# One 64x128 weight load and matmul in place of two 64x64 side by side, in a relu-squared attention followed by a GeGLU feed-forward

## The chip, the core and the metric

The kernel runs on one core of a Trainium2 chip. The metric is the device time of one execution in microseconds (us). It takes 410.21 us, the median of 3 runs (409.67 to 410.41). Matrix products run on TensorE (PE in the profile, its weight loads PEld), elementwise work on VectorE (DVE) and ScalarE (ACT), and most DMAs are issued from GpSimd (POOL) and SyncE (SP).

## The reference

Inputs are float32; the kernel casts to bfloat16 on load and sums in float32.

```python
# q, k, v: (8, 12, 448, 64)   w_gate, w_val: (768, 1536)   w_out: (1536, 768)
scores = (q @ k.T) / sqrt(64)                  # per batch and head, 448 x 448
attn   = maximum(scores, 0)**2 / 448
x      = (attn @ v), heads side by side        # (8*448, 768)
g, val = x @ w_gate, x @ w_val                 # (3584, 1536) each
out    = (gelu(g) * val) @ w_out               # (3584, 768), float32
```

## The kernel before

**Four quarter arrays.** Nearly all products go through the helper `mm` (line 249), which issues one `nc.tensor.matmul` with `tile_position=(64*row, 64*col)`. Weights are 64 rows by 64 columns, so the 128x128 array is used as four independent 64x64 tiles. `row` says which half of the 128 contraction rows (SBUF partitions) an instruction reads, `col` which half of the output partitions it writes. The text calls the two values of `row` the lower and the upper row half. Each matmul comes with one weight load of the same 64x64.

**The products.** For each batch b:

- *scores* (`add_scores`): a unit holds 64 keys for two heads, one head in each row half. Moving data is 448 queries (or 2 x 224). The two columns of a row half have different weights. The result `sp` is squared after a relu by ACT and DVE into `attnT`.
- *values* (`add_values`): one unit for a pair of heads. The two columns of a row half hold different heads, so both weights and moving data differ. The lower half runs seven steps, of two matmuls each, and the upper half seven more, later, onto the same PSUM bank. DVE scales the result into `xT`.
- *gate and value* (`add_gate_value`): for each 128 columns `fc` of the 1,536 and for gate (g=0) and value (g=1), six steps `dc` in the lower row half and six in the upper. A step is two matmuls, j = 0 and 1, which have the same moving data `xT[b][HALF[r], dc, :]` (448 tokens) and the two 64-column halves of the weight.
- *output* (`add_product`): seven products ("1" to "7") for each group of four 64-token chunks instead of eight, with sums of `uT` and of `w_out` made by DVE. The stationary operand is `uT` or a sum of it, two 64-token chunks in the two columns, and the moving data is 384 columns of the weight, the same for j = 0 and 1. There are 7 chunks of 64 tokens in a batch, so that in 4 of the 28 pairs of chunks the two belong to different batches and lie in different `uT` tiles.

Besides, in the first 43 us, the queries and keys of batches 0 and 1 are transposed on the PE with 128-row, 64-column tiles (lines 477 and 514); line 1082 warms the PE up with tiles of that shape, and before 30 us idle time is filled with 128x128 matmuls on constants (`fill`, line 435). Batches 2 to 7 are transposed by DMA.

**The order of the PE's work.** A planner (`run_plan`) with a cost for each operation writes out one order for the PE. It has two streams: PE0 for the lower row half and PE1 for the upper. Gate, value, output and values units go in with `then`: the upper half's steps follow after the lower half's, while the lower half already runs another unit. Scores units go in with `both`: the two row halves run them together. So at most times the two row halves are in different units, and often in different kinds of product. `wait_lower` lets the first upper step of a unit wait for the last lower one, since both add into the same bank. The planner's costs for a step (0.189 us for 448 columns, 0.1625 us for 384) aren't changed by the diff, and neither is the order that it makes.

## Time and profile before

| | |
|---|---|
| median of 3 runs | 410.21 us (409.67 to 410.41) |
| the profiled execution: its time, and its span from first to last instruction | 410.71 us, 408.7 us |
| PE busy | 397.6 us (97%), 8,693 matmuls recorded |
| PEld busy | 357.4 us (87%), 8,696 weight loads |
| DVE, ACT, POOL busy | 250.4, 224.8, 74.3 us |
| matmuls of gate and value / output / scores / values | 4,608 / 2,352 / 768 / 768 |
| granted TensorE clock, mean | 0.998 |

The profiled execution took 2.0 us more than its span and 0.5 us more than the median. The four quarter tiles run side by side, so that the busy time of a group (its union over time) is far less than its count by its mean; and a matmul's recorded duration (349 ns for 448 columns) includes its way through the array. How much PE time a step costs is read from the distance between the starts of two successive matmuls of one tile, 0.19 us for 448 columns.

### The profile page before, as it was taken

The numbers are of one execution on the slowest core, as the hardware profiler recorded it, in microseconds if no ns is written. First come the engines' busy times: TensorE is split into PE (matmuls) and PEld (weight loads), VectorE is DVE, ScalarE is ACT, GpSimd is POOL, SyncE is SP. The second block draws the span as 40 slices with busy tenths as digits, with TensorE's granted clock in tenths as the row PEclk, the third lists the DMA queues.
The fourth block names the chain that finished last, engine by engine and source line by source line (L and its number), as shares of the span: only waits on it lengthen the run. The fifth ranks groups of instructions, "written<-read, shape, count | busy, mean of one in ns | idle before, by whom it ended". The sixth has DMA issues, their size and how long they took to land.

```text
span 408.7 us, 18873 instructions
## 1 busy us (share of the span) xinstructions
PE 397.6 (97%) x8693; PEld 357.4 (87%) x8696; DVE 250.4 (61%) x422; ACT 224.8 (55%) x323; POOL 74.3 (18%) x120
## 2 busy tenths in 40 slices
PE   7899999999999999999999999999999999999993
PEld 3466889988998999999999999999999999999993
DVE  3886678666775757756668563776577464524251
ACT  5858762366757647677266752766456762222220
POOL 8655410203122122001310113200310000000000
PEclk9999999999999999999999999999999999999999
DMA  7999997889769898473995549954993400050005
GB/s 102 189 199 199 198 209 129 117 126 129 108 81 182 148 139 111 58 189 49 116 126 83 143 56 130 113 103 82 107 135 89 116 2 3 3 152 9 3 3 156
DMA packets 75279, 44.87 MB, mean 110 GB/s; under 512 B 36160, under 2 KB 71744, under 8 KB 75200
## 3 DMA queue, kind: packets, MB, share of 16 engines
q0 software_dynamic: 37152, 24.39, 45.1%
q1 hardware_dynamic: 37888, 19.08, 23.7%
q8 instruction: 68, 1.11, 1.2%
q10 hardware_dynamic: 160, 0.20, 0.2%
q14 instruction: 11, 0.09, 0.1%
HBM read 48.76 MB, written 11.01 MB: 146 GB/s over the span
## 4 chain that ended last, share of the span: by engine, by line
PE 94%; DMA 3%; POOL 1%; issue 0%; DVE 0%; ACT 0%; DVEq 0%; POOLq 0%
PE ff L249 84%; PE sp L249 8%; DMA qk<-in_k_dram 2%; DMA v<-in_v_dram 2%; POOL qk L303 1%; PE sp L514 1%; PE ff L435 1%; PE ff L514 1%; DVE uT L721 0%; ACT osb L899 0%; POOL ident masks.py:199 0%; POOL ident masks.py:197 0%; DVEq L721 0%; POOLq L1118 0%
## 5 line engine op out<-in xcount | busy, mean ns | idle before, releaser
L249 PE MATMUL ff<-xT,wv 64*64 64x448 bf16 x2304 | 251.6, 349 | 0.0
L249 PE MATMUL ff<-xT,wg 64*64 64x448 bf16 x2304 | 246.5, 349 | 0.0
L581 ACT ACTIVATE rl<-sp 128x896 bf16<-128x896 f32 x168 | 151.8, 919 | 64.0 <-PE sp L249 62.1
L249 PEld LDWEIGHTS <-wv 64*64 64x64 bf16 x2304 | 147.9, 106 | 10.8
L249 PEld LDWEIGHTS <-wg 64*64 64x64 bf16 x2304 | 147.7, 106 | 9.6
L721 DVE TENSOR_TENSOR uT<-gel,ff 128x448 bf16<-128x448 bf16 x96 | 59.5, 620 | 77.7 <-PE ff L249 67.7
L592 DVE TENSOR_TENSOR attnT<-rl 128x1792 bf16<-128x1792 bf16 (+1 forms) x98 | 92.3, 954 | 24.1 <-ACT rl L581 23.5
L716 ACT ACTIVATE gel<-ff 128x448 bf16<-128x448 f32 x96 | 52.0, 542 | 74.5 <-PE ff L249 73.5
L249 PEld LDWEIGHTS <-s 64*64 64x64 bf16 x1344 | 85.0, 107 | 2.1
L249 PE MATMUL ff<-attnT,v 64*64 64x448 bf16 (+1 forms) x768 | 83.5, 326 | 0.5 <-DMA v<-in_v_dram 0.4
L249 PE MATMUL sp<-qkT 64*64 64x448 bf16 (+1 forms) x768 | 75.2, 328 | 0.8 <-ACT qkT L485 0.6
L249 PE MATMUL ff<-wt,s 64*64 64x384 bf16 x672 | 64.4, 323 | 0.0
L249 PEld LDWEIGHTS <-uT 64*64 64x64 bf16 x1008 | 63.5, 107 | 0.8
L249 PE MATMUL ff<-wo,uT 64*64 64x384 bf16 x672 | 60.9, 323 | 0.0
L249 PE MATMUL ff<-wo,s 64*64 64x384 bf16 x672 | 57.6, 323 | 0.0
L249 PEld LDWEIGHTS <-v 64*64 64x64 bf16 x768 | 46.2, 107 | 4.4 <-issue 0.9
L899 ACT COPY osb<-ff 128x384 f32<-128x384 f32 x56 | 26.6, 478 | 35.5 <-PE ff L249 35.4
L249 PEld LDWEIGHTS <-qkT 64*64 64x64 bf16 x768 | 36.7, 106 | 7.0 <-issue 3.4
L318 POOL DMA_DIRECT2D v<-in_v_dram x48 | 30.1, 634 | 62.0 <-DVE uT L721 38.1
L648 DVE TENSOR_SCALAR xT<-ff 128x448 bf16<-128x448 f32 x48 | 29.9, 623 | 16.0 <-PE ff L249 15.6
L249 PE MATMUL ff<-wt,uT 64*64 64x384 bf16 x336 | 35.3, 323 | 0.0
L897 DVE TENSOR_TENSOR osb<-ff,osb 128x384 f32<-128x384 f32 x42 | 23.3, 556 | 17.4 <-PE ff L249 17.0
(36 smaller groups left out, 126.5 us busy)
## 6 DMA issues: line engine op xcount, KB each, us to landing
out_dram<-osb SPq DMA_DIRECT2D x54, 192.0 KB, 4.1
v<-in_v_dram POOLq DMA_DIRECT2D x48, 128.0 KB, 4.7
qk<-in_q_dram POOLq DMA_DIRECT2D x23, 224.0 KB, 5.4
qk<-in_k_dram POOLq DMA_DIRECT2D x23, 224.0 KB, 5.0
wg<-in_moe_w_gate_dram POOLq DMA_DIRECT2D x6, 384.0 KB, 10.6
wv<-in_moe_w_val_dram POOLq DMA_DIRECT2D x6, 384.0 KB, 11.6
wo<-in_moe_w_out_dram POOLq DMA_DIRECT2D x4, 576.0 KB, 14.9
qkT<-qkr SPq DMA_TRANSPOSE x36, 4.9
```

Source lines behind the costliest of these rows:

```text
L249: return nc.tensor.matmul(o, lhsT, rhs, start=start, stop=stop, skip_group_check=onto, tile_position=(P * row, P * col))
L303: op = load(4 * (h1 - h0) * S * D, lambda: nc.gpsimd.dma_start(tile_of(), src[b, h0:h1].rearrange("h (p c) d -> p h (c d)", c=SC)), deps, ...
L318: return nc.gpsimd.dma_start(v16[b, m][HALF[i], :, :, :], v[b, h0:h1].rearrange("h (p c) d -> p h c d", c=SC)[:, :, c0:c0 + VC, :])
L435: nc.tensor.matmul(t[:, :], warm[:, 0:128], warm[:, :], start=True, stop=True)
L514: nc.tensor.transpose(t[HALF[j], c, :], src[:, 2 * r + j, c, :], ident[:, :], tile_position=(0, P * j))
L581: nc.scalar.activation(duo["rl"][:, u % 2, :, :], box[0][:, :, 0:S], AF.Relu)
L592: nc.vector.tensor_tensor(a[:, part], duo["rl"][:, part], duo["rl"][:, part], op=ALU.mult)
L648: nc.vector.tensor_scalar_mul(xT[b][:, pr, :], box[0][:, 0:S], scalar1=out_scale)
L716: nc.scalar.activation(gel[b, fc][:, :], box[0][:, 0:S], AF.Gelu)
L721: u_op[b, fc].ins = nc.vector.tensor_tensor(uT[b][:, fc, :], gel.pop((b, fc))[:, :], box[0][:, 0:S], op=ALU.mult).ins
L897: ins = nc.vector.tensor_tensor(o, box[0][:, 0:OGS], o, op=ALU.add)
L899: ins = nc.scalar.copy(o, box[0][:, 0:OGS])
```

## The change

The two matmuls j = 0 and 1 of a gate, value or output step become one with a weight of 64 rows by 128 columns at column 0, which writes all 128 output partitions. The moving data, the PSUM banks, the sums and the order stay as they are. Output steps whose two chunks belong to different batches stay two matmuls of 64x64, since their stationary operand isn't one slice. Scores and values stay as they are.

```diff
 # add_gate_value, emit(r, dc)
-            for j in range(2):
-                ins = mm(box[0][HALF[j], 0:S], w[HALF[r], dc, o + P * j:o + P * (j + 1)],
-                         xT[b][HALF[r], dc, :], r, j, r == 0 and dc == 0, r == 1 and dc == KC - 1)
-            box[1] = ins
+            box[1] = mm(box[0][:, 0:S], w[HALF[r], dc, o:o + 2 * P],
+                        xT[b][HALF[r], dc, :], r, 0, r == 0 and dc == 0, r == 1 and dc == KC - 1)
 # add_product, emit(r, fc)
-            for j in range(2):
-                if isinstance(source, str):
-                    a = st["tile"][source][HALF[r], fc, HALF[j]]
+            if isinstance(source, str):
+                parts = [(slice(0, 2 * P), st["tile"][source][HALF[r], fc, :])]
+            else:
+                t, half = source
+                (b, c), (b1, _) = chunks[t]
+                if b == b1:
+                    parts = [(slice(0, 2 * P), uT[b][HALF[r], half * KH + fc, c * P:(c + 2) * P])]
                 else:
-                    t, half = source
-                    b, c = chunks[t][j]
-                    a = uT[b][HALF[r], half * KH + fc, c * P:(c + 1) * P]
-                ins = mm(box[0][HALF[j], 0:OGS], a, weight_of(name, fc)[HALF[r], :], r, j,
+                    parts = [(HALF[j], uT[b][HALF[r], half * KH + fc, c * P:(c + 1) * P])
+                             for j, (b, c) in enumerate(chunks[t])]
+            for j, (to, a) in enumerate(parts):
+                ins = mm(box[0][to, 0:OGS], a, weight_of(name, fc)[HALF[r], :], r, j,
```

## The prediction

> **What bounds the kernel now.** I read the page's busy times and the chain first, then the stages.

> ```profile
> PE 397.6 (97%) x8693; PEld 357.4 (87%) x8696; DVE 250.4 (61%) x422; ACT 224.8 (55%) x323; POOL 74.3 (18%) x120
> PE   7899999999999999999999999999999999999993
> PEclk9999999999999999999999999999999999999999
> PE 94%; DMA 3%; POOL 1%; issue 0%; DVE 0%; ACT 0%; DVEq 0%; POOLq 0%
> 100.00:200.00 100.00, 99.99 (x2266) 93.54 (x2263) 67.72 (x110) 64.62 (x91) 18.02 (x30) 1.00 0.76 117
> 335.00:400.00 65.00, 65.00 (x1474) 61.24 (x1467) 29.02 (x61) 16.86 (x32) 0.00 (x0) 1.00 0.10 27
> ```

> The last two lines are stages: length, then PE, PEld, DVE, ACT, POOL, granted clock, DMA. The PE bounds everything but the first 30 us, at full clock; no other engine is above two thirds in a stage. But a busy PE may be only partly filled, so I asked what the four tiles do inside it. The timeline of the PE (start, length, what, count; neighbours of one kind merged):

> ```profile
> 60.89 0.35 PE L249 MATMUL ff<-xT,wg 64*64 64x448 bf16 x2
> 60.98 0.38 PE L249 MATMUL ff<-xT,wv 64*64 64x448 bf16 x2
> 61.08 0.35 PE L249 MATMUL ff<-attnT,v 64*64 64x448 bf16 x2
> 61.17 0.38 PE L249 MATMUL ff<-xT,wv 64*64 64x448 bf16 x2
> 61.27 0.35 PE L249 MATMUL ff<-attnT,v 64*64 64x448 bf16 x2
> ```

> One row half runs gate/value (60.98, 61.17), the other another unit (60.89, 61.08, 61.27), each 0.19 us a step, two matmuls per step. Successive starts of output steps are 0.162 us apart (108.46, 108.62, 108.78), those of transposes of 128 columns 0.055, so a column streams in some 0.42 ns and the constant per matmul is 2 to 3 ns. With that price all 8,696 matmuls, four side by side (two for 128x64, one for 128x128), fill 387 us of the 408.7. From 100 to 400 us the tiles are over 99% filled: there is no hole to close.

> **What the change removes.** Of 4,608 gate/value and 2,352 output matmuls all but 144 are paired: batches meet inside a pair of chunks in 4 of 28 pairs; two of these are the first pair of their group, in products 1 and 2, two the second, in product 4, so (2+2+1+1) products x 24 matmuls. That leaves 3,408 fewer matmuls and as many fewer loads (8,696 to 5,288). It takes nothing off the path: a 64x128 matmul streams the same 448 or 384 columns and holds both tiles of its row half for the same 0.189 or 0.162 us. Issue isn't the limit (where four are ready they start within 0.01 us, as at 42.54), and loads lie under the matmuls. The wider load is bounded by the transposes: two 64-column loads every 0.055 us, so 128 columns in at most that, under 0.162. Zero, as long as loads are issued ahead. Waits, DMAs, other engines and the order don't move.

> **What it adds.** Until now all PE work after 43 us had one shape. Afterwards scores, values and straddling output steps are 64x64 and the rest 64x128. What does a change of shape cost? This trace has such changes early on, between 64x64 and 128x64 or 128x128:

> ```profile
> 41.17 0.35 PE L249 MATMUL ff<-xT,wv 64*64 64x448 bf16 x2
> 41.17 0.35 PE L249 MATMUL ff<-attnT,v 64*64 64x448 bf16 x2
> 41.36 0.35 PE L249 MATMUL ff<-xT,wv 64*64 64x448 bf16 x2
> 41.64 0.97 PE L514 MATMUL sp<-ident,qk 128*64 128x128 bf16 x28
> 42.54 0.38 PE L249 MATMUL ff<-xT,wv 64*64 64x448 bf16 x2
> 42.55 0.38 PE L249 MATMUL ff<-attnT,v 64*64 64x448 bf16 x2
> 42.76 0.35 PE L249 MATMUL ff<-xT,wg 64*64 64x448 bf16 x2
> ```

> The last 64x64 pair (41.36) has streamed its columns by 41.55; the transposes begin at 41.64, 0.09 later. Their group ends at 42.61; the last of 0.22 began at 42.39 and streamed by 42.44; the next 64x64 begins at 42.54, 0.10 later. It isn't a late input: loads, which otherwise start as the matmul before them starts, also first start at 41.64 and 42.54. Behind four 128x128 fills (12.44 to 13.48, the last begun at 13.10 and streamed by 13.31) the next 64x64 begins at 13.41, again 0.10 later. After the change the first step is 0.214 long instead of 0.189 (42.54 to 42.76): 0.025 of weight load lies bare (0.011 for 128x128). So a change of shape costs 0.092 + 0.025 = 0.117 us, in which all four tiles stand still, and from one change to the next instructions of one shape alone run.

> The order in which the kernel issues its matmuls, which the change keeps, has 36 changes of shape now and 1,042 with the pairs joined. The 1,006 new ones: 285 of the narrow runs are a values step or two of one row half, between wide steps of the other; some 130 are scores. Two terms:

> - standstill: 1,006 x 0.117 = 117.7 us;
> - lost overlap: a values step in one row half ran beside a gate step in the other; now they take turns. Adding up, run by run of one shape, the fill of its busiest tile gives 389.4 us now and 457.2 with the pairs joined: 67.8 us. As a check, some 300 values steps of (6 x 0.189 + 2 x 0.095)/8 = 0.166 us each alone make 50 us, about 63 straddling output steps of 0.162 another 10, and ragged ends of wide runs the rest.

> Sum 185.5 us, nearly all before 335 us: 906 of the changes come before the last scores, 46 behind the last values. On the profiled execution's 410.7 it makes 596.2, on the median 595.7; I take 596. Nothing covers it: the PE sets the end, and others, 250 us busy at most, only wait longer.

> No row shows a change of columns alone at 64 rows, so the price has bounds: from below nothing (if this isn't such a change), from above the row just used, with a bare load between 0 and 0.1 us (a recorded 128-column load takes 0.097): 0 and +160 to +225. A gain is excluded, since no row shows a column in under 0.42 ns. I take the upper end: the rows nearest to it, the same instructions in the same queue, show a stop both on going narrower and on going wider.

> [...]

> **Rivals.**

> *The stop holds only the row half that changes.* The 128-row shapes use both halves, so the rows above can't exclude that a column change stops one alone. Followed half by half, the order has 705 more changes, each 0.117 us in one of two halves that otherwise run on: 705 x 0.117 / 2 = 41 us; a walk through the order, halves waiting for each other's place, gives 47, or 36 without bare loads. Time 447 to 458, taken 458. For it: the halves keep their own pace (0.162 beside 0.189).

> *No stop for columns (not slower).* Only a joining or splitting of the row halves would empty the array; 64x64 and 64x128 in one half would follow each other as now. Price: 0.117 becomes 0. Place: all 1,006 changes. It decides if a change costs under 0.8 us / 1,006 = 0.8 ns. Then 410.2; two tiles that drift 0.03 us apart (60.98 shows 0.38 for a pair) would move together, worth 0.03 us at a unit's end, at most 1 us in all. Against it: loads in these rows weren't even prefetched.

> *Wide loads bound the steps.* If the two row halves' 128-column loads went one after the other at the recorded 0.106, a pair of steps would need 0.213: 1,152 gate/value steps per half x 0.024 + 624 output steps x 0.051 = +59 us, 470. Against it: the transposes' 0.055 for 128 columns.

> **How the numbers follow.** Standstill of the whole array 0.66 (596, its own range 571 to 635); one row half 0.16 (458); no stop 0.14; loads 0.04 (470). About 0.2% is what a measurement of this kernel can tell from no change, 0.8 us: of the no-stop case 0.09 falls within, 0.03 faster, 0.02 slower. Faster 0.03, same 0.09, slower 0.88. Range 445 to 635: it takes in the row-half and load cases and leaves out the no-stop case (0.14) and some tail.

> **What would show it.** In the profile of the changed kernel: 5,288 loads; a mixed stretch where a wide step's start comes 0.09 after the columns before it have streamed, with its load starting no earlier; a values pair never within a wide matmul's stream; PEld idle rising; a granted clock still at 1; the last 46 us of wide work growing only some 10 us (46 changes) to 56. If in the timeline values and gate steps still alternate at 0.09 us as at 60.89 to 61.27, the prediction is wrong, and if they do so with pauses in one half only, the row-half rival is right.

## The result and the profile after

The changed kernel takes 606.4 us (median of 4 runs, 603.18 to 608.17) against 410.3 before: 1.477 times as long, 95% interval 1.470 to 1.485. The profiled execution took 608.17 us, with a span of 606.3. 596 was predicted. Two things were not as told: the array clock did not stay at 1 (0.962 in the mean of the profiled execution), and the standstills were a little cheaper than priced.

From the page of the changed kernel: busy times and counts, PE and granted clock in 40 slices, and two groups (busy, mean ns | idle before).

```profile
PE 596.6 (98%) x5285; PEld 260.5 (43%) x5288; DVE 253.4 (42%) x422; ACT 228.0 (38%) x323; POOL 73.8 (12%) x120
PE   7999999999999999999999999999999999999996
PEclk9979999999859999999999999999998799999999
L249 PE MATMUL ff<-xT,wv 64*128 64x448 bf16 x1152 | 265.9, 352 | 0.0
L249 PEld LDWEIGHTS <-wv 64*128 64x128 bf16 x1152 | 94.8, 94 | 62.3 <-issue 32.0
```

5,288 loads are left, as counted. The PE still reads 98% busy, and DVE and ACT run as many instructions as before; PE busy time grew by 199 us while its instructions fell by 39%. Busy time hides what happened; the timeline of the PE in a mixed stretch shows it (start, length, what, count):

```profile
262.90 0.38 PE L249 MATMUL ff<-attnT,v 64*64 64x448 bf16 x2
262.91 0.56 PE L249 MATMUL sp<-qkT 64*64 64x448 bf16 x4
263.40 0.36 PE L249 MATMUL ff<-xT,wg 64*128 64x448 bf16 x1
263.69 0.38 PE L249 MATMUL ff<-attnT,v 64*64 64x448 bf16 x2
264.00 0.36 PE L249 MATMUL ff<-xT,wg 64*128 64x448 bf16 x1
264.00 0.50 PE L249 MATMUL ff<-wo,s 64*128 64x384 bf16 x2
264.20 0.35 PE L249 MATMUL ff<-xT,wg 64*128 64x448 bf16 x1
```

Before, gate and values steps of the two row halves started 0.09 us apart and overlapped. Now the gate step at 263.40 runs alone, the values step at 263.69 alone, the gate step at 264.00 with an output step of the other half, because both are wide. From 263.40 a step streams until 263.59, and the next shape starts at 263.69, 0.10 later; likewise 263.69, 263.88 plus a bare load, 264.00. The weight loads of the same stretch:

```profile
263.40 0.09 PEld L249 LDWEIGHTS <-wg 64*128 64x128 bf16 x1 [0.36 <-issue]
263.69 0.11 PEld L249 LDWEIGHTS <-v 64*64 64x64 bf16 x2 [0.20 <-issue]
263.99 0.09 PEld L249 LDWEIGHTS <-wg 64*128 64x128 bf16 x1 [0.20 <-issue]
```

No load is issued ahead across a change of shape, here or at any other at full clock in this trace: the first load of the new shape starts no sooner than 0.09 us after the columns before it have streamed. Where nothing changes, wide steps keep their pace, both halves at once:

```profile
101.32 0.35 PE L249 MATMUL ff<-xT,wv 64*128 64x448 bf16 x1
101.32 0.35 PE L249 MATMUL ff<-xT,wg 64*128 64x448 bf16 x1
101.51 0.35 PE L249 MATMUL ff<-xT,wv 64*128 64x448 bf16 x1
101.51 0.35 PE L249 MATMUL ff<-xT,wg 64*128 64x448 bf16 x1
```

The new part is the clock. Two stages of 50 us each (length, PE, PEld, DVE, ACT, POOL, granted clock, DMA):

```profile
100.00:150.00 50.00, 50.00 (x449) 22.01 (x445) 22.07 (x35) 21.77 (x31) 6.73 (x11) 1.00 0.58 90
150.00:200.00 50.00, 50.00 (x373) 19.14 (x371) 18.99 (x32) 18.20 (x25) 5.56 (x10) 0.80 0.47 76
```

In the second the PE is as busy, at a mean clock of 0.80, and issues 76 matmuls fewer. The trace's clock record has three stretches at half clock before the end, 10.2, 20.5 and 13.7 us long, 44.4 us in all; before there was none while the PE worked. The four executions follow their clock: 608.2 and 608.1 us at 0.962 and 0.965, 604.8 at 0.968, 603.2 at 0.971.

### The profile page after: what moved, and what is told of

It is laid out like the page before. It is cut to its first block, busy times and chain, and to the rows that moved or that the text cites. A ratio compares the mean times of both kernels' runs of the same rounds, so it can differ in the third digit from the quotient of the medians.

```text
span 606.3 us, 12047 instructions
## 1 busy us (share of the span) xinstructions
PE 596.6 (98%) x5285; PEld 260.5 (43%) x5288; DVE 253.4 (42%) x422; ACT 228.0 (38%) x323; POOL 73.8 (12%) x120
## 4 chain that ended last, share of the span: by engine, by line
PE 97%; DMA 1%; POOL 1%; issue 0%; ACT 0%; POOLq 0%
PE ff L249 87%; PE sp L249 9%; DMA qk<-in_k_dram 1%; PE sp L514 1%; POOL qk L303 0%; PE ff L435 0%; PE ff L514 0%; ACT osb L901 0%; POOL ident masks.py:199 0%; POOL ident masks.py:197 0%; POOLq L1120 0%
## 5 line engine op out<-in xcount | busy, mean ns | idle before, releaser
L249 PE MATMUL ff<-xT,wv 64*128 64x448 bf16 x1152 | 265.9, 352 | 0.0
L249 PE MATMUL ff<-xT,wg 64*128 64x448 bf16 x1152 | 263.4, 355 | 0.0
L249 PE MATMUL ff<-attnT,v 64*64 64x448 bf16 (+1 forms) x768 | 127.2, 358 | 0.1
L249 PEld LDWEIGHTS <-wv 64*128 64x128 bf16 x1152 | 94.8, 94 | 62.3 <-issue 32.0
L249 PEld LDWEIGHTS <-wg 64*128 64x128 bf16 x1152 | 93.9, 94 | 61.2 <-issue 31.7
L249 PE MATMUL ff<-wt,s 64*128 64x384 bf16 x336 | 74.9, 339 | 0.0
L249 PEld LDWEIGHTS <-s 64*128 64x128 bf16 x672 | 55.9, 96 | 39.8 <-issue 25.3
L249 PEld LDWEIGHTS <-v 64*64 64x64 bf16 x768 | 39.3, 106 | 77.9 <-issue 76.8
L249 PE MATMUL sp<-qkT 64*64 64x448 bf16 (+1 forms) x768 | 70.5, 353 | 1.1 <-ACT qkT L485 0.6
L249 PE MATMUL ff<-wo,uT 64*128 64x384 bf16 (+1 forms) x384 | 69.9, 330 | 0.0
L249 PE MATMUL ff<-wo,s 64*128 64x384 bf16 x336 | 64.3, 336 | 0.0
L249 PEld LDWEIGHTS <-uT 64*128 64x128 bf16 (+1 forms) x576 | 42.1, 98 | 36.1 <-issue 26.4
L249 PE MATMUL ff<-wt,uT 64*128 64x384 bf16 (+1 forms) x192 | 46.1, 375 | 0.0
L249 PEld LDWEIGHTS <-qkT 64*64 64x64 bf16 x768 | 21.9, 104 | 52.9 <-issue 50.6
L318 POOL DMA_DIRECT2D v<-in_v_dram x48 | 29.6, 622 | 102.1 <-DVE uT L719 62.9
## 6 DMA issues: line engine op xcount, KB each, us to landing
wg<-in_moe_w_gate_dram POOLq DMA_DIRECT2D x6, 384.0 KB, 10.2
```

The lines of the kernel that those rows point to most:

```text
L249: return nc.tensor.matmul(o, lhsT, rhs, start=start, stop=stop, skip_group_check=onto, tile_position=(P * row, P * col))
L318: return nc.gpsimd.dma_start(v16[b, m][HALF[i], :, :, :], v[b, h0:h1].rearrange("h (p c) d -> p h c d", c=SC)[:, :, c0:c0 + VC, :])
```

## Experiments

Five readings were at stake: a change of shape stops the whole array (the forecast); it stops only the row half that changes; column changes stop nothing; wide weight loads bound the steps; or each wide instruction is slower in itself (196 us / 3,408 = 0.058 each). Full-clock figures in the expectations use the price measured in the changed kernel's trace, 0.111 us for a change.

**The shapes by themselves.** A kernel with only PE work, in stretches of one pattern each. `narrow(r)` is two 64x64 side by side in row half r (0 is the lower), `wide(r)` one 64x128:

```diff
+    for i in range(100):    # C; A has narrow(0), narrow(1) and B wide(0), wide(1)
+        narrow(0, i % 8)
+        wide(1, i % 8)
+    ...                     # D to H likewise
```

> PE work alone, nothing of the reference is computed (the output is zeros): eight stretches of steps of 448 columns, one after the other. Steps take 0.189 us. A: 64x64 pairs, lower and upper half, 100 times; B: 64x128, both halves, 100 times; C: 64x64 pair in the lower half, 64x128 in the upper, 100 times; D: 64x64 in both halves, then 64x128 in both, 100 times; E: 200 times 64x128 in the lower half alone; F: 64x128 in both halves, then 128x128, 60 times; G: 64x64 in both halves, then a pair of 128x64, 60 times; H: a pair of 128x64, then 128x128, 60 times. Theory (a change of shape stops the whole array, some 0.094 us plus a bare load of 0.011 to 0.025): A 18.9, B 18.9, C 200 x 0.300 = 60, D 200 x 0.300 = 60, E 37.8, F and H some 35, G 36.7. Rival (the stop holds only the row half that changes): C 18.9, since neither half changes, D 60. Rival (no stop when only columns change): C 18.9, D 37.8, F 35, G 36.7, H 22.7. Rival (wide loads bound the steps): B 21 or more.

Three parts of its PE timeline: C at full clock, C later, and D:

```profile
56.20 0.36 PE L48 MATMUL hi<-x,w 64*128 64x448 bf16 x1
56.49 0.38 PE L44 MATMUL lo<-x,w 64*64 64x448 bf16 x2
56.80 0.36 PE L48 MATMUL hi<-x,w 64*128 64x448 bf16 x1
57.09 0.38 PE L44 MATMUL lo<-x,w 64*64 64x448 bf16 x2
...
70.08 0.55 PE L48 MATMUL hi<-x,w 64*128 64x448 bf16 x1
70.56 0.58 PE L44 MATMUL lo<-x,w 64*64 64x448 bf16 x2
71.08 0.55 PE L48 MATMUL hi<-x,w 64*128 64x448 bf16 x1
...
161.68 0.36 PE L48 MATMUL lo<-x,w 64*128 64x448 bf16 x1
161.69 0.36 PE L48 MATMUL hi<-x,w 64*128 64x448 bf16 x1
161.98 0.38 PE L44 MATMUL lo<-x,w 64*64 64x448 bf16 x2
161.98 0.38 PE L44 MATMUL hi<-x,w 64*64 64x448 bf16 x2
```

In C neither row half ever changes its shape: the lower is always 64x64, the upper always 64x128. Yet they take turns: 0.60 us from one wide step to the next, so 0.300 for a step and a change, 0.111 more than a step. That excludes the row-half rival and the no-stop rival at once. D has the same 0.60 a round with both halves filled. The joining of columns at 128 rows (H) and that of rows with columns kept (F, G) took 0.30 to 0.31 too. A and B each took 19.0 us for their 100 rounds: wide steps are no slower, at 0.19 us in both halves, and the last two readings fall as well.

The stages A, B, C at half clock, D at full clock and E (wide steps in the lower half alone):

```profile
17.83:36.87 19.04, 19.04 (x401) 11.61 (x401) 0.00 (x0) 0.00 (x0) 1.00 0.85 335
36.87:55.89 19.02, 19.02 (x204) 9.65 (x200) 0.00 (x0) 0.00 (x0) 1.00 0.01 2
60.80:152.00 91.20, 91.20 (x276) 21.14 (x274) 0.00 (x0) 0.00 (x0) 0.50 0.00 0
160.00:215.00 55.00, 55.00 (x546) 18.84 (x544) 0.00 (x0) 0.00 (x0) 1.00 0.00 1
216.00:254.00 38.00, 38.00 (x204) 18.80 (x201) 0.00 (x0) 0.00 (x0) 1.00 0.00 0
```

(Length, PE, PEld, DVE, POOL, granted clock, DMA.) Five microseconds into C the clock halved and stayed there until 7 us into D: a round of C then took 1.00 us (70.08 to 71.08). E keeps half the array streaming all the time (0.5 of it), D, from 159.8 us on, the whole array 0.63 of the time; both ran at full clock. C streams half the array 0.63 of the time, 0.31. So what the clock follows isn't the busy PE, at 100% in all three.

**Everything wide.** Scores merged, and values, score tails and straddling output steps doubled, so that no narrow shape is left after the transposes (here the last are at 48 us):

```diff
 # add_values, on top of the change; scores and straddling steps likewise
-                o = box[0][HALF[j], 0:S]
+                o = box[0][:, 0:S]
...
-                    ins = mm(o, v16[b, pr // 2][HALF[i], 2 * (pr % 2) + j, w + i, :], a, i, j,
+                    ins = mm(o, two(w + i), a, i, 0,      # 128 columns
```

> The changed kernel with every other 64x64 step wide too: scores of 448 columns merged, and the steps whose two columns have different moving data (values, score tails, straddling output steps) as two 64x128 matmuls one after the other, so these stream twice as long. Some operands are then not the reference's (a score's second 64 keys, values' second head), so the output isn't either; sizes, order and everything outside the PE stay. After 43 us no change of shape is left. The tiles' fill grows from 387 to 429 us. Theory (each change of shape stops the whole array): the 1,006 stops and the lost overlap go, 410 + 43 = 453 us, at full clock. Rival (stop in one row half only): 453 as well. Rival (a wide step itself costs more, 196 us / 3,408 = 0.058 each): about 720. Rival (lower clock because of the shape): over 470.

458.44 us (4 runs, 458.24 to 459.24), 1.117 times before (1.112 to 1.121). The array streams 42 us more than in the changed kernel, and the time is 148 us shorter. The forecast's mechanism gives 453; some 5 us are left over. By the trace the time in which any tile streams grew by 49 us where the forecast has 43; why isn't known. The cost of the change thus lies in mixing, not in wide steps. From its page:

```profile
PE 447.6 (98%) x4997; PEld 306.9 (67%) x5000; DVE 252.4 (55%) x422; ACT 226.2 (50%) x323; POOL 73.7 (16%) x120
PEclk9999999999999999999999999999999999999998
```

**Stops without lost overlap.** Only scores wide, in the kernel before:

```diff
 # add_scores, emit(j, pr)
+            if not tail:
+                mm(sp[:, j, 0:S].rearrange("k (c p) -> k c p", c=SC),
+                   t[:, cl, :], t[:, :, HALF[0]], j, 0, True, True)
+                return
```

> The kernel before, with only the 576 score matmuls of 448 columns merged into 288 of 64x128 (the second 64 keys are other columns than the reference's, so the output isn't either). Scores units run in both row halves together, so hardly any overlap is lost: the order has 267 changes of shape more, and the fill of the busiest tile, run by run, grows only from 389.4 to 393.4 us. Theory (whole array): 267 x 0.111 = 29.6 plus 4.0, 444 us. Rival (row half only): 439. Rival (cost by wide instruction, 288 x 0.058): 427. Rival (no stop): 410.

446.19 us, 1.087 times before (1.082 to 1.092), at full clock throughout. Against the 410.97 of the same chip that is 35.2 us for 267 changes, 0.132 each all told, or 0.117 after the 4.0 us of overlap that were expected. Added up from the trace, the time in which any tile streams grew by 8 us, not 4, which leaves 0.10 for each. Either way the standstill is a cost of its own.

**Half of the change.** Gate and value wide, output narrow:

```diff
 # add_product: as before; add_gate_value: as after
```

> Only the gate and value half of the change; output steps stay pairs of 64x64. Fewer instructions are wide (2,304 of 3,408), but output steps now are one more kind that the wide steps alternate with: 1,377 new changes in place of 1,006, and the fill run by run is 497.7 us (457.2 with the whole change, 389.4 before). Theory (whole array): 410 + 153 + 108 = 671 us at full clock, up to 4% more if the clock falls as it did with the whole change: slower than the whole change by 65 to 90. Rival (row half only): 453. Rival (cost by wide instruction): 543, faster than the whole change.

Four executions took 766.1, 767.3, 785.4 and 801.8 us, at granted clocks of 0.853, 0.849, 0.826 and 0.804. The two with the higher clock make 1.867 times before (1.856 to 1.878): a third less of the edit, and 160 us slower than the whole. Its page's clock and a piece of its PE timeline:

```profile
PEclk9999789795785999999778898656999999575998
...
105.75 0.35 PE L249 MATMUL ff<-wo,uT 64*64 64x384 bf16 x2
106.03 0.36 PE L249 MATMUL ff<-xT,wv 64*128 64x448 bf16 x1
106.32 0.35 PE L249 MATMUL ff<-wo,uT 64*64 64x384 bf16 x2
```

Output and gate steps, which overlapped before and overlap again when both are wide, now take turns. The time without the clock was right: with the columns that streamed at half clock counted at full clock, the profiled run's 766.1 becomes 675, and 671 was expected. The 4% allowed for the clock was not: the profiled run had 222 us at half clock. From here I read off the traces when the clock changes; it is an estimate from these runs, and the expectations call it the clock rule. In the changed kernel every stretch between two changes of the clock is a whole multiple of 3.41 us: 10.2, 122.9, 20.5, 283.3, 13.7 and 126.3 us are 3, 36, 6, 83, 4 and 37 of them. I cut the traces into windows of that length and added up from the matmuls the share of the array that streams in each. Here the clock fell after windows of 0.32 to 0.38 and came back after windows of 0.74 or more; in the changed kernel it fell after 0.31, 0.33 and 0.34, came back after 0.85, 0.92 and 0.94, and stayed at one half after ten windows of 0.36 to 0.69. Two further parts of the change put that rule to the test beforehand.

> Only the output half of the change; gate and value steps stay pairs of 64x64. 1,104 instructions are wide. The order gets 1,011 new changes of shape, about as many as with the whole change, and the fill run by run is 475.4 us (457.2 there). Theory (each change stops the whole array for 0.111 us, and only one shape runs between): 410 + 112 + 86 = 609 us at full clock. With the clock rule read from the runs so far (half clock after a window of 3.41 us in which less than about 0.37 of the array streamed, full clock after one with over about 0.77), walked through the order: 712 to 751, about 735, since output steps in one row half alternate with gate steps in the other for long stretches. So slower than the whole change although two thirds of the edit are left out. Rival (stop in one row half only): 437. Rival (cost by wide instruction, 0.058 each): 474.

> Only the value half of the gate and value units is made wide; gate and output steps stay 64x64. 1,152 instructions are wide, a third of the whole change. Gate and value units alternate, so that most of the time one row half would run a wide and the other a narrow unit: 2,042 new changes of shape, fill run by run 567 us. Theory (whole array): 410 + 227 + 178 = 815 us at full clock; with the clock rule (half after a window under about 0.37, full after one over about 0.77) 1,070 to 1,150. Theory without the clock rule, at the clock share of the whole change: about 840. Rival (stop in one row half only): 457. Rival (cost by wide instruction): 477.

```diff
 # output_only: add_gate_value as before, add_product as after
 # value_only: add_product as before; in add_gate_value
+            if g == 1:
+                box[1] = mm(box[0][:, 0:S], w[HALF[r], dc, o:o + 2 * P], ...
+            else:                        # two of 64x64, as before
```

Output only: 754.5 us (2 runs, 753.7 and 755.3); 712 to 751 was expected. Value only: 1,186.7 us (2 runs, 1,183.7 and 1,189.8), 2.89 times before with a third of the edit; 1,070 to 1,150 was expected. Their pages:

```profile
PE 744.6 (99%) x7592; PEld 343.8 (46%) x7592; DVE 252.6 (34%) x422; ACT 227.1 (30%) x323; POOL 73.8 (10%) x120
PEclk9999658956558958579785797557985598765998
...
PE 1178.4 (99%) x7544; PEld 373.5 (31%) x7544; DVE 253.0 (21%) x422; ACT 229.2 (19%) x323; POOL 73.9 (6%) x120
PEclk9965555555955558755579555655558855675557
```

(The first two lines are output only, the last two value only.) The size and the order of both are as the walk through the issue order with the clock rule has them; without the rule they would be 609 and 815, and with half-clock columns counted at full clock the profiled runs give 613 and 829. Both times lie above their ranges, by 0.5% and 3%, so the rule is coarse.

**More of the change.** Scores wide as well:

```diff
 # the changed kernel, with the scores of the diff above
```

> The whole change, and the 576 score matmuls of 448 columns merged too (the second 64 keys are other columns than the reference's, so the output isn't either). More is wide, and less alternates: 817 new changes instead of 1,006, fill run by run 455.2 instead of 457.2 us. Theory (whole array): 567 us at full clock, with the clock rule 579 to 591, so some 20 us faster than the whole change. Rival (stop in one row half only): 434. Rival (cost by wide instruction): slower than the whole change by 17.

583.2 us (2 runs, 580.9 and 585.5), inside the 579 to 591: 189 changes fewer and 23 us less. More wide instructions made it faster.

**The same price in the kernel before.** The transposes of batch 1 as quarters:

```diff
 # add_transposes, b = 1 (the views of the bank and of the copy are left out here)
+                for c in range(SC):
+                    for i in range(2):
+                        for j in range(2):
+                            nc.tensor.transpose(t[HALF[j], i, c, :],
+                                qk16[b, m][HALF[i], 2 * r + j, c * D:(c + 1) * D],
+                                ident[HALF[i], HALF[i]], tile_position=(P * i, P * j))
```

> The kernel before, all 64x64 from 26 us on: the transposes of batch 1 (84 matmuls of 128x64 on 128 columns, in four groups between 27 and 43 us) become 168 of 64x64 on 64 columns, row half by row half, into one PSUM bank each. It takes 8 changes of shape off the bound stretch. Theory (whole array): 8 x 0.111 = 0.9 us, and ragged row halves at each of them, 0.1 to 0.2 us each: 0.8 to 2 us faster, 408.5 to 409.5 us, where the transposes themselves stay as long. Rival (the stop there was for joining the row halves and later work waits for the DMAs of that stretch anyway): no change. Rival (64-column streams are shorter than their weight loads): up to 1 us slower.

413.6 us, 1.0065 times before (1.0039 to 1.0091): 0.65% slower, against the theory's 0.8 to 2 us faster. The stops did go (the steps around the quarters follow each other at once), but the PE now stands idle at three places, put to "issue", that is to no semaphore in the profile:

```profile
PE sp L249 <- issue: 2.1, 1, 2.1
PE ff L249 <- issue: 1.0, 1, 1.0
PE sp L514 <- issue: 0.7, 1, 0.7
```

Together 3.8 us, at 33, 39 and 44 us; the kernel before has none there. In that stretch the DMA engines move 198 GB/s in both kernels. The 16 KB blocks of the queue for instructions (68 and 1.11 MB on the page of the kernel before) land at the same times in both (31.4, 37.5, 43.6 us), while this kernel has 168 PE instructions more and works through them sooner. By the counts, an estimate, the PE ran out of instructions. The kernel before has 17,416 PE records and 68 such blocks, so a block would hold some 256 instructions; between one of the three stops and the next the PE ran 256 instructions, both times, and each time it went on 1.3 to 1.5 us after a block had landed in full (32.34, 38.48 and 44.54; 33.86, 39.78 and 45.98). No run takes this wait away. In the profiled run the clock was also at one half for 3.4 us behind the longest stop (46.8 to 50.2). The gain of about 1 us that the theory gives may be there beneath it, but isn't shown.

## Why the prediction was right, step by step

- *The change removes nothing from the path.* Right: wide steps of one shape run at 0.19 us in both halves, and A and B took the same 19.0 us.
- *1,006 new changes of shape.* Right: in the order of the weight loads, all of which are recorded, the trace before has 35 changes and the trace after 1,041. The planner's order was the thing to count.
- *0.117 us for each.* Slightly too high. In the trace after, from the streamed columns to the next shape is 0.092 (wide to narrow) or 0.095 us; the first narrow step is longer by 0.024, but the first wide one only by 0.011. The mean is 0.111, which C gives too; 111.7 us instead of 117.7. That a change of columns alone would cost what the 128-row shapes cost was taken from the nearest rows of the trace before; C shows it for 64x64 against 64x128, across both row halves (0.60 us a round, where A and B took 0.19).
- *67.8 us of lost overlap.* Right. With 0.417 ns a column (at half clock in the trace after, steps of 384 columns start 320 ns apart, 0.833 a column) and half-clock columns counted at full clock, the time in which at least one tile streams is 390.9 us in the trace before and 460.2 in the trace after, 69.3 more. Gate and value only has 108.3 more, with 108 expected.
- *59 us for the rival of the wide loads.* Its 0.106 is the record of a 64-column load, where the prediction itself has 0.097 for 128 columns, and 552 output steps of a half are wide, not 624. A wide load measures 0.094, two of them 0.188, less than a step of 448 columns.
- *The granted clock still at 1.* Wrong; this is the step that failed. The prediction gave no reason for it and had no term for the clock, though by its own sum the array stands empty for 118 us. In C a half-clock round goes 0.60/1.00 as far in the same time, so 44.4 us of it lose 40%, an estimate of 17.8 us; counted by the columns that streamed at half clock in the trace after, it is 18.2.

The sum with the measured terms: 410.7 + 111.7 + 67.8 + 17.8 = 608.0, against a profiled 608.2. The two traces by themselves say the same: from the first column to the last it takes 198.0 us longer, of which 69.3 are lost overlap, 18.2 the clock and 110.5 a standing array. So the forecast's 596 was 6 us too high on the standstill and 18 too low on the clock; that it came within 2% owes a little to luck, since the two errors have opposite signs. The range of 445 to 635 would have held the row-half rival too; it is C and the timeline that decide between the two, not the time. The last 46 us of wide work behind the last values grew as forecast, from 47 us (355.3 to 402.5) to 56 (544.3 to 600.5).

## What to carry to other kernels

Merging two tiles of the array was free here only where everything that ran beside it in time had the merged shape too (0.19 us a round of B, 0.60 of C): count the changes of shape in the issue order, not the instructions saved, since a third of this edit cost four times as much as the whole. A PE that reads 98% busy may be standing still nearly a fifth of the time (110.5 us of 606): look at the distance between starts and at whether loads are issued ahead. Add up the share of the array that streams, because here the clock seems to follow that (one half in C at 0.31, full in E at 0.5).

## What was not expected of the hardware

In the trace after, a wide load is recorded at 0.094 us and leaves 0.011 bare, a narrow one of half the columns (that of a values step) at 0.106 and 0.024: twice the columns in less time.
